# Masked attention and a top-1 expert layer on one core: the last heads by halves, the third half's rows through DRAM, a new written order

## The chip, the core and the metric

The kernel runs on one core of a Trainium2 chip. A core has a matrix engine (PE, TensorE, with its weight loader PEld), three others for vectors and scalars (DVE, VectorE; ACT, ScalarE; POOL, GpSimd) and a sync engine (SP) that only issues transfers. Each works through its own list of instructions in order, and semaphores make one wait for another. PE writes to PSUM, eight banks of 2 KB per partition; the rest works on SBUF. Transfers run on 16 DMA engines and are issued from the queues of SP, ACT and POOL. The metric is device time in microseconds.

## The reference

Attention on 2 batches of 8 heads, 768 positions of 64 numbers, where a query sees only the keys of its own bucket (six sign bits of a projection). Its output, 768 rows of 512 per batch, goes to a layer of 8 experts: each row to one expert, the argmax of a gate unless a local gate says to keep the expert of the row before.

```python
q_bits = (np.einsum('bhsd,dk->bhsk', q, proj) > 0)
mask = q_bucket[:, :, :, None] == k_bucket[:, :, None, :]
scores = np.where(mask, scale * np.matmul(q, k.transpose(0, 1, 3, 2)), -1e9)
attn = np.exp(scores - scores.max(-1, keepdims=True))
x = np.matmul(attn / (attn.sum(-1, keepdims=True) + 1e-9), v)    # then rows of 8*64
...
e = argmax(logits[b, s]) if s == 0 or local_gate[b, s] < 0.5 else prev_e
h = np.maximum(x[b, s] @ w1[e], 0.0)                             # 512 -> 1024
out[b, s] = p[e] * (h @ w2[e])                                   # 1024 -> 512
```

## The kernel before

**Attention.** Two heads make a pair; there are 8 pairs p (0 to 3 of batch 0, 4 to 7 of batch 1). The queries of a pair fall into two halves of 384, the keys into six tiles kt. For each pair `s1` makes scores for the row maxima (PE, then a reduction on DVE, L268), and `s2.p.kt.half` makes the scores again (PE, L259), with the exponential on ACT (L315). `pv.p.kt.half` multiplies with v (PE, L329), `flat` (L336) adds the term for queries without keys, and `padd` (L322, POOL or DVE) adds up the six exponentials of a half. `sa`/`sb` (L372, L381) turn these sums into denominators for both halves of a pair; in the last pair `sah`/`sbh` do it for one half, with 12 records of one column (L351). `ot`/`oth` copy pv's result to SBUF (ACT) and `ug` multiplies it with the identity and the gate's weights (PE, L414); DVE then normalises it into the row buffer xt and into gr, the gate's parts.

**Route.** The gate's sums (lg), seven small DVE operations (L488 to L495), a transpose `tk` (PE, L505), two scans over positions (DVE, L510 and L512: the expert that is kept, and the running count per expert), a transpose back `tb` (PE, L519) and some fifteen small operations give each row a slot. Rows are scattered by POOL to a DRAM buffer xs, 256 slots per expert (L551), 128 rows at a time. `step` advances this work, which is a generator.

**First expert.** Its 256 slots are not waited for in DRAM. For batch 0 they come from DRAM (`xa`, L639, then `rows`, PE, L708); rows of batch 1 are gathered by matmuls with a one-hot matrix: the third half (batch 1, first half) by `ohe`, `hle`, `ge`, the last half by `oh`, `gl` (L714, 24 matmuls of 256 columns each). `ready` splits the result into high and low parts x0H and x0L, as all products here are made of split operands. `hidden` is an expert's first layer (hps, L756), 24 matmuls for each of four tiles; the second layer is yps (L837).

**What sets the order.** Up to the first expert's input it is written out by hand: the string ORDER lists calls such as `pv.6.3.1`, and the table MOVED says which of two engines or queues a part takes (padd: 0 POOL, 1 DVE; hi: 0 ACT, 1 DVE, 2 POOL; lo: 0 DVE, 1 POOL; wl and split_l: 0 POOL, 1 DVE). From the second expert on a scheduler orders the instructions. For each expert it has eight weight tiles of 512 KB (`weights`, L791 the load, L793 the high part wh on ACT, L794 the low part wl on DVE), the rows (`xprep`: load xsl L800, eight transposes xps L804, xH on ACT L806, xL on DVE), and two scatters to out (L847). In expert 0 the call for expert 1's rows stands in the middle of the second layer, at t=1, i=2; its load is issued from POOL's queue, behind the small load PI.

Of the kernel before, what the change touches and what calls it, by code (L numbers as in the profile page):

```python
# [16 lines left out]
CAP = 256  # L17
# [44 lines left out]
padd.5.5.1 s2.6.3.0 s2.6.2.0 s2.6.4.1 s2.6.0.1 s2.6.2.1 wl.0 s2.6.1.1 padd.5.5.0 padd.6.2.0 s2.6.3.1 s1.7.4.1
padd.6.1.1 pv.6.0.0 pv.6.0.1 padd.6.3.0 pv.6.2.1 s1.7.5.1 s1.7.2.1 mf.6 s1.7.2.0 pv.6.1.1 pv.6.2.0 padd.6.4.0 pv.6.4.0
sa.5 ve.1 ma.7 mb.7 we.1 ug.4 sb.5 mc.7 padd.6.2.1 flat.6.0 flat.6.1 ug.5 mf.7 step.0 split_h.0 s2.7.2.0 s2.6.5.1
padd.6.3.1 we.2 ve.0 s2.7.0.0 s2.7.1.0 s2.6.5.0 padd.7.1.0 s2.7.3.0 padd.7.2.0 padd.6.4.1 padd.6.5.0 split_h.1
pv.6.4.1 pv.6.3.0 wh.2 padd.7.3.0 padd.6.5.1 pv.6.1.0 pv.6.5.0 we.4 pv.6.3.1 wh.1 pv.6.5.1 ot.6 s2.7.4.0 s2.7.2.1
padd.7.4.0 s2.7.1.1 s2.7.5.0 s2.7.0.1 sa.6 pv.7.0.0 flat.7.0 wl.2 step.0 split_l.0 we.5 split_l.1 padd.7.5.0 step.0
sb.6 wh.5 ug.6 xa.0 pv.7.2.0 pv.7.1.0 padd.7.1.1 padd.7.2.1 pv.7.4.0 pv.7.3.0 pv.7.5.0 sah.7.0 wl.1 oth.7.0 sbh.7.0
ugh.7.0 step.1 s2.7.3.1 s2.7.4.1 padd.7.3.1 padd.7.4.1 s2.7.5.1 xa.1 step.1 pv.7.0.1 flat.7.1 pv.7.2.1 padd.7.5.1
pv.7.4.1 pv.7.1.1 split_h.2 pv.7.3.1 step.1 pv.7.5.1 sah.7.1 wh.4 step.1 sbh.7.1 ohe oth.7.1 ugh.7.1 late step.2  # L70
rows.2 hle.0 split_h.3 split_l.2 rows.0 rows.1 hle.1 step.2 split_l.3 ge.0 rows.3 ge.1 ve.3 ge.2 step.2 oh step.2 wl.5
wl.4 ve.2 ge.3 gl.0 gl.1 ready.0 gl.2 gl.3 ready.1
"""

MOVED = {
    "bd": {(1, 0, 1): 1, (3, 0, 0): 1, (3, 0, 1): 1, (3, 1, 1): 1, (4, 0, 0): 1, (4, 1, 1): 1, (5, 0, 0): 1, (5, 0, 1): 1, (5, 1, 0): 1, (5, 1, 1): 1, (6, 0, 0): 1, (6, 0, 1): 1, (6, 1, 0): 1, (7, 1, 0): 1, (7, 1, 1): 1},
    "hi": {(3, 1): 1, (4, 1): 1, (5, 0): 1},
    "hle": {(1,): 1},
    "lo": {(0, 0): 1, (0, 1): 1, (1, 0): 1, (1, 1): 1, (2, 0): 1, (3, 1): 1, (4, 0): 1, (4, 1): 1, (5, 1): 1, (6, 0): 1, (7, 0): 1, (7, 1): 1},
    "lx": {(1, 1): 1, (2, 0): 1, (4, 0): 1, (5, 1): 1, (7, 0): 1},  # L80
    "padd": {(0, 1, 1): 1, (0, 4, 1): 1, (1, 3, 0): 1, (1, 5, 1): 1, (2, 2, 1): 1, (2, 4, 1): 1, (3, 1, 0): 1, (3, 4, 1): 1, (3, 5, 0): 1, (4, 1, 1): 1, (4, 4, 0): 1, (4, 5, 0): 1, (5, 1, 0): 1, (5, 5, 1): 1, (6, 5, 0): 1, (6, 5, 1): 1, (7, 1, 0): 1, (7, 1, 1): 1, (7, 2, 0): 1, (7, 2, 1): 1, (7, 3, 0): 1, (7, 3, 1): 1, (7, 4, 0): 1, (7, 4, 1): 1, (7, 5, 0): 1, (7, 5, 1): 1},
    "split_l": {(0,): 1, (1,): 1, (2,): 1, (3,): 1},
    "wl": {(0,): 1, (1,): 1, (2,): 1, (3,): 1, (4,): 1, (5,): 1},
}


LEFT = {0: (), 1: ()}
# [45 lines left out]
def tile_kernel(ctx, tc, qT, kT, v, proj, wg, w1, w2, cst, out):  # L133
    nc = tc.nc
    const = ctx.enter_context(tc.tile_pool(name="const", bufs=1))
    dram = ctx.enter_context(tc.tile_pool(name="dram", bufs=1, space=bass.MemoryType.DRAM))
    pvp = ctx.enter_context(tc.tile_pool(name="pvp", bufs=1, space=PSUM, reuse_waits="tile"))
    actx = ExitStack()
    ptp = actx.enter_context(tc.tile_pool(name="ptp", bufs=10))
    own = actx.enter_context(tc.tile_pool(name="own", bufs=1))  # L140
# [221 lines left out]
    def ot(p):  # L362
        for half in range(2):
            oth(p, half)
# [572 lines left out]
```

## Time and profile before

| | us |
|---|---|
| time, median of 3 runs (437.73 to 438.17) | 437.81 |
| the profiled execution | 437.44 |
| its span | 435.6 |
| PE busy | 420.4 (97%) |
| DVE busy | 286.2 (66%) |
| ACT busy | 207.1 (48%) |
| POOL busy | 175.6 (40%) |
| mean granted clock | 0.997 |

The span is the time from the first to the last instruction of the profile; the rest of the profiled execution's own time lies around it. Busy times are sums over the whole span and say little about one stage: attention takes the first 230 us, the route and the first expert's input the next 14, the experts the rest, one every 22.8 us at the end. Durations on PE overlap, since matmuls are pipelined; what one costs is the distance between starts.

### The profile page before, as it was taken

How to read it: one execution, taken by the hardware profiler on the slowest of the kernel's cores; microseconds unless marked ns; L12 is line 12 of the kernel's file. 1: busy time of each engine (PE TensorE's matmuls, PEld its weight loads, DVE VectorE, ACT ScalarE, POOL GpSimd, SP SyncE). 2: the span in 40 equal slices, each digit the busy share in tenths (PEclk: the TensorE clock that was granted, in tenths of full speed). 3: DMA queues.
4: the chain of work that ended last, by engine and by line, in shares of the span. 5: the costliest groups of instructions: out<-in, count | busy, mean ns of one | idle time of the engine just before them, and what ended most of it. 6: DMA issues, size and time to landing. Idle time of an engine off the chain costs nothing.

```text
span 435.6 us, 8104 instructions
## 1 busy us (share of the span) xinstructions
PE 420.4 (97%) x3206; PEld 328.6 (75%) x3206; DVE 286.2 (66%) x454; ACT 207.1 (48%) x288; POOL 175.6 (40%) x126
## 2 busy tenths in 40 slices
PE   7999999999999999999997998999999999999993
PEld 5665766747676675767656997989898989898992
DVE  3878858586665797779698865968574746464110
ACT  4444542715644364436532346756673746463110
POOL 4573886397579749792074212020000000000001
PEclk9999999999999999999999999999999999999998
DMA  8451224012122350203034179997777767740100
GB/s 267 117 169 31 89 78 129 19 42 87 45 80 66 110 175 5 63 2 110 2 147 169 55 244 367 362 325 256 251 260 242 227 216 239 241 154 2 38 2 32
DMA packets 42612, 60.08 MB, mean 138 GB/s; under 512 B 5431, under 2 KB 25129, under 8 KB 42572
## 3 DMA queue, kind: packets, MB, share of 16 engines
q1 hardware_dynamic: 38835, 50.14, 35.8%
q0 software_dynamic: 2432, 6.84, 4.2%
q10 hardware_dynamic: 1305, 2.57, 1.9%
q8 instruction: 26, 0.43, 0.4%
q14 instruction: 14, 0.11, 0.1%
HBM read 47.75 MB, written 11.56 MB: 136 GB/s over the span
## 4 chain that ended last, share of the span: by engine, by line
PE 49%; issue 40%; POOL 5%; DVE 1%; DMA 1%; ACT 1%; POOLq 0%; SPq 0%
PE s L259 25%; PE pv L329 15%; POOL out L847 4%; PE ug L414 3%; PE st L372 1%; PE hb L198 1%; POOL xs L551 1%; DMA xk<-kT 1%; PE pv L336 1%; PE st L381 1%; PE busy L605 1%; PE vt L584 0%; POOL xhl L646 0%; DMA PI<-xs 0%; PE st L351 0%
## 5 line engine op out<-in xcount | busy, mean ns | idle before, releaser
L268 DVE TENSOR_REDUCE mx<-s 128x2 f32<-128x768 f32 x96 | 88.8, 954 | 30.6 <-PE s L259 30.2
L794 DVE TENSOR_TENSOR wl<-st,wh 128x1024 fp32r<-128x1024 f32 x56 | 67.3, 1222 | 49.9 <-ACT wh L793 49.1
L315 ACT ACTIVATE pt<-s 128x768 f32<-128x768 f32 x96 | 71.6, 813 | 52.5 <-PE s L259 52.4
L322 POOL TENSOR_TENSOR sp<-sp,pt 128x768 f32<-128x768 f32 x44 | 82.1, 1877 | 26.9 <-DVE sp L322 20.2
L793 ACT ACTIVATE wh<-st 128x1024 fp32r<-128x1024 f32 x56 | 58.5, 1058 | 32.9 <-DMA st<-w 21.7
L259 PE MATMUL s<-hx 64*128 64x384 f32 x384 | 71.1, 365 | 0.5 <-DVE mx L268 0.3
L329 PE MATMUL pv<-pt,v 128*64 128x384 f32 x384 | 70.3, 496 | 0.0
L847 POOL DMA_INDIRECT out<-y,xsl x13 | 13.3, 1024 | 139.2 <-ACT y L840 139.2
L259 PE MATMUL s<-b,b 64*128 64x384 f32 x372 | 63.3, 334 | 0.6 <-ACT b L222 0.6
L259 PEld LDWEIGHTS s<-hx 64*128 64x128 f32 x384 | 36.4, 184 | 25.1 <-issue 8.7
L756 PE MATMUL hps<-xH,wh 128*128 128x256 f32 x224 | 53.8, 277 | 0.0
L756 PE MATMUL hps<-xH,wl 128*128 128x256 f32 x224 | 53.8, 277 | 0.0
L837 PE MATMUL yps<-wh,hH 128*128 128x512 f32 (+1 forms) x136 | 52.2, 384 | 0.0
L837 PE MATMUL yps<-wh,hL 128*128 128x512 f32 (+1 forms) x136 | 51.7, 380 | 0.0
L837 PE MATMUL yps<-wl,hH 128*128 128x512 f32 (+1 forms) x136 | 51.5, 379 | 0.0
L329 PEld LDWEIGHTS pv<-pt,v 128*64 128x64 f32 x384 | 24.2, 136 | 30.8 <-issue 29.9
L756 PEld LDWEIGHTS hps<-xH,wl 128*128 128x128 f32 x224 | 42.1, 188 | 0.3
L756 PEld LDWEIGHTS hps<-xH,wh 128*128 128x128 f32 x224 | 42.1, 188 | 0.3
L259 PEld LDWEIGHTS s<-b,b 64*128 64x128 f32 x372 | 35.5, 185 | 0.8 <-ACT b L222 0.8
L759 DVE SCALAR_TENSOR_TENSOR hL<-hps,hH 128x512 fp32r<-128x512 f32 x32 | 22.0, 687 | 19.3 <-ACT hH L758 19.3
L756 PE MATMUL hps<-xL,wh 128*128 128x256 f32 x224 | 34.6, 277 | 0.0
L259 PE MATMUL s<-hx,lx 64*128 64x384 f32 x192 | 32.7, 333 | 0.0
(204 smaller groups left out, 628.4 us busy)
## 6 DMA issues: line engine op xcount, KB each, us to landing
st<-w SPq DMA_DIRECT2D x56, 512.0 KB
xs<-z SPq DMA_DIRECT2D x8, 513.0 KB
st<-w SPq DMA_DIRECT2D x13, 256.0 KB
xsl<-xs SPq DMA_DIRECT2D x6, 514.0 KB
v<-v SPq DMA_DIRECT2D x12, 256.0 KB
xk<-kT SPq DMA_DIRECT2D x6, 384.0 KB
xq<-qT SPq DMA_DIRECT2D x5, 384.0 KB
xq<-qT ACTq DMA_DIRECT2D x3, 384.0 KB
```

The source lines that it names most:

```text
L259: nc.tensor.matmul(out=sc[:, h, 0:384], lhsT=w[r, cols[0]], rhs=x[r, cols[1]], tile_position=(64 * h, 0), start=first and n == 0, stop=las ...
L268: nc.vector.tensor_reduce(out=MX[p][:, kh, i // 3, :, i % 3], in_=sc[:, :, 0:384], axis=AX.X, op=ALU.max)
L315: nc.scalar.activation(out=pt.rearrange("p (a q) -> p a q", a=2), in_=sc[:, :, 0:384], func=ACTF.Exp, scale=0.125)
L322: eng.tensor_tensor(out=SP[p, h], in0=PT[p, 0, h] if kt == 1 else SP[p, h], in1=PT[p, kt, h], op=ALU.add)
L329: nc.tensor.matmul(out=PV[p][64 * h:64 * h + 64, half, 0:384], lhsT=V[b, kt][:, pp * 128 + 64 * h:pp * 128 + 64 * h + 64], rhs=PT[p, kt, h ...
L414: nc.tensor.matmul(out=t[:, half, j * 146:j * 146 + 146], lhsT=OT[p][:, q * 128:q * 128 + 128], rhs=iw[:, pp])
L756: nc.tensor.matmul(out=hps[:, k], lhsT=w, rhs=x, start=(k, n) in ends[0], stop=(k, n) in ends[1])
L759: LAST["DVE"] = nc.vector.scalar_tensor_tensor(out=hL, in0=hps, scalar=0.0, in1=hH.bitcast(F32), op0=ALU.max, op1=ALU.subtract).ins
L793: nc.scalar.activation(out=H, in_=st, func=ACTF.Copy)
L794: nc.vector.tensor_tensor(out=L, in0=st, in1=H.bitcast(F32), op=ALU.subtract)
L837: nc.tensor.matmul(out=yps[:, us], lhsT=h[:, k, ts], rhs=w[:, k, us], start=(n == 0), stop=(n == 23))
L847: i = nc.gpsimd.indirect_dma_start(out=dst, out_offset=bass.IndirectOffsetOnAxis(ap=idx, axis=0), in_=y[:, us], in_offset=None, bounds_che ...
```

## The change

- **pv.** The PSUM tile of a pair (two banks, one buffer) becomes one tile of one bank per half (two buffers).
- **Last pairs.** Pairs 6 and 7 go by halves: (6,0) and (7,0) first, then (6,1) and (7,1). Their sums are made by group, `sc` and `sd` for GROUPS, in place of sa.6, sb.6, sah, sbh. `pre` sums the gate's first six parts ahead.
- **Third half.** Its rows are scattered to DRAM early enough for `xa`; `ohe`, `hle`, `ge` (24 gathers) go. The matmuls of `rows` and `gl` share a helper `into`.
- **Route of the last half.** Scans in pieces of 256 and 128 columns (`sn`), back transposes and copies in two parts (`bk`, `cp`), the one-hot by parts (`oh.j`). The late normalisation moves from one DVE operation to six on ACT.
- **Expert 1's rows.** They are loaded by POOL's queue before PI (`rows1`), and `xprep` does them in two parts at t=1, i=3. Its PSUM tile has a pool of its own.
- **ORDER and MOVED** are new throughout. padd on DVE 26 → 37 of 80, hi on DVE 3 → 10, lo on POOL 12 → 16, wl on DVE 6 → 4.

Of ORDER one line is shown.

```diff
+GROUPS = (((6, 0), (7, 0)), ((6, 1),), ((7, 1),))
...
+pre.0 ugh.7.0 s2.6.5.1 s2.6.4.1 step.1 padd.6.4.1 pv.6.0.1 padd.6.5.1 pv.6.2.1 pv.7.0.1 step.1 split_l.0 s2.7.4.1
...
+    pvp = pctx.enter_context(tc.tile_pool(name="pvp", bufs=2, space=PSUM, reuse_waits="tile"))
...
-    def sah(p, half):
-        st = ps.tile([128, 2, 512], F32, tag="big", name="st")
-        ST[p, half] = st
-        terms = [SP[p, half]] + [PT[p, kt, half] for kt in LEFT[half]]
-        for h in range(2):
-            for j in range(3):
-                for n, x in enumerate(terms):
-                    nc.tensor.matmul(out=st[:, 0, 3 * h + j:3 * h + j + 1], lhsT=x[:, h * 384 + 128 * j:h * 384 + 128 * j + 128],
-                                     rhs=ones[:, 0:1], start=(n == 0), stop=(n == len(terms) - 1))
-
-    def sbh(p, half):
-        d = ST[p, half][:, 1, 0:6].rearrange("p (h j) -> p h j", h=2)
-        nc.vector.scalar_tensor_tensor(out=d, in0=DN[p][:, half], scalar=1e-9,
-                                       in1=ST[p, half][:, 0, 0:6].rearrange("p (h j) -> p h j", h=2), op0=ALU.add, op1=ALU.add)
-        if p not in DR:
-            DR[p] = smp.tile([128, 2, 2, 3], F32, tag="r", name="r")
-        nc.vector.reciprocal(out=DR[p][:, half], in_=d)
-
-    def ot(p):
-        for half in range(2):
-            oth(p, half)
+        nc.scalar.activation(out=OT[p][:, half * 384:half * 384 + 384], in_=PV[p, half][:, 0:384], func=ACTF.Copy)
+
+    def sc(g):
+        ST["g", g] = st = ps.tile([128, 2, 512], F32, tag="big", name="st")
+        n = 0
+        for p, half in GROUPS[g]:
+            for h in range(2):
+                nc.tensor.matmul(out=st[n:n + 32, 0, 0:384], lhsT=ones, rhs=SP[p, half][:, h * 384:h * 384 + 384], tile_position=(0, n))
+                n += 32
+        ss = smp.tile([128, 384], F32, tag="ss", name="ss", bufs=1)
+        nc.scalar.activation(out=ss[0:n], in_=st[0:n, 0, 0:384], func=ACTF.Copy)
+        NF["g", g] = ss
+
+    def sd(g):
+        st, ss, m = ST["g", g], NF["g", g], len(GROUPS[g])
+        n = 64 * m
+        for j in range(3):
+            nc.tensor.transpose(st[:, 1, j * n:j * n + n], ss[0:n, j * 128:j * 128 + 128], idf[0:n, 0:n])
+        d = st[:, 1, 384:384 + 6 * m].rearrange("p (a h j) -> p a h j", a=m, h=2)
+        r = smp.tile([128, 2, 2, 3], F32, tag="r", name="r")
+        for a, (p, half) in enumerate(GROUPS[g]):
+            nc.vector.scalar_tensor_tensor(
+                out=d[:, a], in0=DN[p][:, half], scalar=1e-9,
+                in1=st[:, 1, 0:3 * n].rearrange("p (j a h r) -> p a h j r", j=3, a=m, h=2)[:, a, :, :, 0],
+                op0=ALU.add, op1=ALU.add)
+            DR[p, half] = r[:, a]
+        nc.vector.reciprocal(out=r[:, 0:m].rearrange("p a h j -> p (a h j)"), in_=d.rearrange("p a h j -> p (a h j)"))
...
+        def scan(i, a, c1, c2):
+            h = halves[i]
+            o, p = slice(384 * h + c1, 384 * h + c2), 384 * h + c1 - 1
+            if a == 0:
+                V_.tensor_tensor_scan(out=E[:, o], data0=KS[i][:, c1:c2], data1=cs[0:8, 3:4].to_broadcast([8, c2 - c1]),
+                                      initial=E[:, p:p + 1] if h or c1 else 0.0, op0=ALU.subtract, op1=ALU.is_lt)
+            else:
+                V_.tensor_tensor_scan(out=C[:, o], data0=E[:, o], data1=E[:, o], op0=ALU.add, op1=ALU.max,
+                                      initial=C[:, p:p + 1] if h or c1 else CU[0] if b else cs[0:8, 152:153])
+
+        def back(q1, q2):
+            for a, src in enumerate((E, C)):
+                for q in range(q1, q2):
+                    o = 384 * halves[0] + 128 * q
+                    nc.tensor.transpose(tb[:, a, q * 8:q * 8 + 8], src[:, o:o + 128], idf[0:8, 0:8])
+
+        def copy(q1, q2):
+            V_.tensor_copy(out=EC[b][:, :, q0 + q1:q0 + q2], in_=tb[:, :, q1 * 8:q2 * 8].rearrange("p a (q e) -> p a q e", e=8))
...
-    def ohe():
-        OHE.append(onehot("sp", 0))
...
-    def hle(i):
-        c = slice(256 * i, 256 * i + 256)
-        hl = [ptp.tile([128, 3, 256], F32R, tag="pt", name="xhl") for _ in range(2)]
-        HLE.append(hl)
-        nc.scalar.activation(out=hl[0], in_=XT[1][:, 0:3, c], func=ACTF.Copy)
-        (nc.vector, nc.gpsimd)[moved("hle", i)].tensor_tensor(
-            out=hl[1], in0=XT[1][:, 0:3, c], in1=hl[0].bitcast(F32), op=ALU.subtract)
...
+    def into(c, cols, **kw):
+        i = c // 2
+        if not xt0:
+            for k in range(2):
+                xt0[k], XN[k] = pvp.tile([128, 512], F32, tag="pv", name="xt0").rearrange("p (c n) -> p c n", c=2), 0
+        nc.tensor.matmul(out=xt0[i][:, c % 2, cols], start=XN[i] == 0, stop=XN[i] == 15, **kw)
+        XN[i] += 1
...
+    def gl(c, j):
+        for k in range(2):
+            into(c, slice(0, 256), lhsT=XHL[k][:, j, 128 * c:128 * c + 128], rhs=OH[0][:, j])
...
+    def late():
+        t, r = LATE.pop()
         for j in range(3):
-            for k in range(2):
-                nc.tensor.matmul(out=xt0[c // 2][:, c % 2], lhsT=hl(k, j), rhs=oh[:, j], start=False,
-                                 stop=(last and c % 2 == 1 and j == 2 and k == 1))
-
-    def ge(c):
-        gather(OHE[0], c, lambda k, j: HLE[c // 2][k][:, j, 128 * (c % 2):128 * (c % 2) + 128])
-
-    def gl(c):
-        gather(OH[0], c, lambda k, j: XHL[k][:, j, 128 * c:128 * c + 128], True)
-
-    def oh():
-        OH.append(onehot("oh", 3))
-
-    def late():
-        LATE.pop()()
+            for h in range(2):
+                nc.scalar.activation(out=XT[1][:, 3 + j, 384 + 64 * h:448 + 64 * h], in_=t[:, 1, 146 * j + 64 * h:146 * j + 64 * h + 64],
+                                     func=ACTF.Copy, scale=r[:, h, j:j + 1])
...
+        rows1 = xload(mp, xs[CAP:2 * CAP], nc.gpsimd)
+        nc.gpsimd.dma_start(out=PI, in_=xs[0:CAP, 512:514].rearrange("(t p) c -> p t c", p=128))
...
-    def xprep(slots, queue=nc.sync, after=None):
-        xsl = mp.tile([128, 2, 514], F32, tag="xsl", name="xsl")
-        with tc.issue_after(after) if after else nullcontext():
-            queue.dma_start(out=xsl, in_=slots.rearrange("(t p) c -> p t c", p=128))
-        xps = pvp.tile([128, 4, 256], F32, tag="pv", name="xps")
-        for c in range(4):
-            for t in range(2):
-                nc.tensor.transpose(xps[:, c, 128 * t:128 * t + 128], xsl[:, t, 128 * c:128 * c + 128], idf)
+    def xprep(xsl, parts=1):
+        xps = px.tile([128, 4, 256], F32, tag="xps", name="xps")
         xH, xL = (wide(mp, [128, 4, 256], n, XOFF, 64) for n in ("xH", "xL"))
-        LAST["x"] = (nc.scalar.activation(out=xH, in_=xps, func=ACTF.Copy).ins,
-                     nc.vector.tensor_tensor(out=xL, in0=xps, in1=xH.bitcast(F32), op=ALU.subtract).ins)
-        return xsl[:, :, 512:514], xH, xL
+        LAST["x"] = []
+        for part in range(parts):
+            cs_ = slice(4 // parts * part, 4 // parts * (part + 1))
+            for c in range(4)[cs_]:
+                for t in range(2):
+                    nc.tensor.transpose(xps[:, c, 128 * t:128 * t + 128], xsl[:, t, 128 * c:128 * c + 128], idf)
+            LAST["x"] += (nc.scalar.activation(out=xH[:, cs_], in_=xps[:, cs_], func=ACTF.Copy).ins,
+                          nc.vector.tensor_tensor(out=xL[:, cs_], in0=xps[:, cs_], in1=xH[:, cs_].bitcast(F32), op=ALU.subtract).ins)
+            yield xsl[:, :, 512:514], xH, xL
...
-                if after and (t, i) == (1, 2):
-                    nxt = mid()
                 for k in range(2):
+                    if after and (t, i) == (1, 3):
+                        nxt = next(prep)
```

In the places that follow, rows of the order are of one engine. First PE around the end of attention, before: st is a sum, ug the projection, xt the first expert's rows being put together, tk and tb the route's transposes.

```order
L351 MATMUL st<-ones,sp 128x1 x6
L414 MATMUL ug<-iw,ot 128x146 x3
L708 MATMUL xt_3001<-cs,xa 128x128 x2
L708 MATMUL xt_3010<-cs,xa 128x128 x4
L505 MATMUL tk<-cs,gr_115 8x128 x3
L714 MATMUL xt_3010<-oh,xhl 128x256 x6
L708 MATMUL xt_3001<-cs,xa 128x128 x2
L714 MATMUL xt_3010<-oh,xhl 128x256 x6
L714 MATMUL xt_3001<-oh,xhl 128x256 x6
L519 MATMUL tb<-cs,rE 128x8 x3
L519 MATMUL tb<-cs,rC 128x8 x3
L714 MATMUL xt_3001<-oh,xhl 128x256 x6
```

And now, from sd.1 on:

```order
L360 MATMUL st<-cs,ss 128x64 x3
L350 MATMUL st<-sp,ones 32x384 x2
L419 MATMUL ug<-iw,ot 128x146 x3
L360 MATMUL st<-cs,ss 128x64 x3
L419 MATMUL ug<-iw,ot 128x146 x3
L517 MATMUL tk<-cs,gr_115 8x128 x3
L722 MATMUL xt_3009<-cs,xa 128x128 x2
L534 MATMUL tb<-cs,rE 128x8 x2
L534 MATMUL tb<-cs,rC 128x8 x2
L722 MATMUL xt_3009<-cs,xa 128x128 x2
L534 MATMUL tb<-cs,rE 128x8
L534 MATMUL tb<-cs,rC 128x8
L722 MATMUL xt_3010<-cs,xa 128x128 x4
```

The gathers of the third half (xhl) are gone, and with them the one-column sum; two half projections and three small sums stand ahead of tk. The matmuls on xa now stand behind tk and ahead of tb.

Second, ACT at expert 1, before. wh are weight tiles of expert 1 in the order of their loads by number (3404, 3410, 3416, 3422 of w1, 3544, 3550 of w2), xH its rows, y the output of expert 0.

```order
L793 ACTIVATE wh_3410<-st_3408 128x1024
L840 ACTIVATE y_3337<-yps_3312,PI_112 128x512
L806 ACTIVATE xH_3366<-xps_3357 128x1024
L793 ACTIVATE wh_3416<-st_3414 128x1024
L793 ACTIVATE wh_3544<-st_3542 128x1024
L840 ACTIVATE y_3382<-yps_3342,PI_112 128x512
L793 ACTIVATE wh_3422<-st_3420 128x1024
L793 ACTIVATE wh_3550<-st_3548 128x1024
L758 ACTIVATE hH_3451<-hps_3426 128x512
```

And now (3396, 3402, 3408, 3414 of w1; 3536, 3542, 3548, 3554 of w2):

```order
L826 ACTIVATE wh_3402<-st_3400 128x1024
L880 ACTIVATE y_3329<-yps_3304,PI_112 128x512
L826 ACTIVATE wh_3536<-st_3534 128x1024
L839 ACTIVATE xH_3354<-xps_3353 128x512
L826 ACTIVATE wh_3542<-st_3540 128x1024
L880 ACTIVATE y_3374<-yps_3334,PI_112 128x512
L826 ACTIVATE wh_3548<-st_3546 128x1024
L839 ACTIVATE xH_3354<-xps_3353 128x512
L826 ACTIVATE wh_3408<-st_3406 128x1024
L826 ACTIVATE wh_3554<-st_3552 128x1024
L826 ACTIVATE wh_3414<-st_3412 128x1024
L789 ACTIVATE hH_3443<-hps_3418 128x512
```

xH comes in two halves. The first tile of w2 has moved ahead of the first half, and the second and third ahead of the second half; the third and fourth tile of w1 come later. DVE's order of wl and xL is the same.

Third, PE at the same place now (before, the eight transposes stood in the middle of the second layer, 12 yps ahead of the first hps):

```order
L877 MATMUL yps<-wh,hL 128x512
L787 MATMUL hps<-xH,wh 128x256
L787 MATMUL hps<-xH,wl 128x256
L787 MATMUL hps<-xH,wh 128x256
L787 MATMUL hps<-xH,wl 128x256
L787 MATMUL hps<-xH,wh 128x256
L787 MATMUL hps<-xH,wl 128x256
L787 MATMUL hps<-xH,wh 128x256
L787 MATMUL hps<-xH,wl 128x256
L838 MATMUL xps<-cs,xsl 128x128 x4
L787 MATMUL hps<-xH,wh 128x256
L787 MATMUL hps<-xH,wl 128x256
```

Eight matmuls use the first half of xH, then four transposes make the second half, and all that follows waits for it.

## Rows read from the trace of the kernel before

**Rows 1.** Windows (start:end, PE, PEld, DVE, ACT, POOL busy, clock, DMA share, GB/s)

```profile
220.00:230.00 10.00, 9.80 (x74) 5.96 (x73) 9.10 (x22) 4.05 (x7) 5.96 (x5) 1.00 0.36 134
...
260.00:270.00 10.00, 8.75 (x48) 7.20 (x47) 4.83 (x5) 5.09 (x6) 1.31 (x1) 1.00 1.03 354
```

**Rows 2.** Timeline of PE near 100 us (start, duration, line, shapes, count, [idle before])

```profile
100.45 0.44 PE L259 MATMUL s<-hx 64*128 64x384 f32 x2
100.73 0.34 PE L259 MATMUL s<-b,b 64*128 64x384 f32 x2
```

**Rows 3.** Timeline of PE, sums, pv runs and projection

```profile
211.41 0.85 PE L372 MATMUL st<-sp,ones 128*32 128x384 f32 x8
212.20 0.87 PE L329 MATMUL pv<-pt,v 128*64 128x384 f32 x4
...
214.59 1.66 PE L414 MATMUL ug<-iw,ot 128*128 128x146 f32 x12
216.17 3.45 PE L329 MATMUL pv<-pt,v 128*64 128x384 f32 x20
219.55 1.50 PE L351 MATMUL st<-ones,sp 128*128 128x1 f32 x12
220.91 0.99 PE L414 MATMUL ug<-iw,ot 128*128 128x146 f32 x6
```

**Rows 4.** Timeline of PE, last pv to first expert

```profile
229.41 0.87 PE L329 MATMUL pv<-pt,v 128*64 128x384 f32 x4
230.21 1.50 PE L351 MATMUL st<-ones,sp 128*128 128x1 f32 x12
...
232.67 1.71 PE L708 MATMUL xt<-cs,xa 128*128 128x128 f32 x12
235.81 0.49 PE L505 MATMUL tk<-cs,gr 128*8 128x128 f32 x3 [1.43 <-DVE gr L495]
...
239.98 0.35 PE L519 MATMUL tb<-cs,rE 8*128 8x8 f32 x3
...
241.35 0.38 PE L714 MATMUL xt<-oh,xh 128*128 128x256 f32 x1
...
244.32 0.86 PE L756 MATMUL hps<-x0H,b 128*128 128x256 f32 x6
```

**Rows 5.** Timeline of DVE, the two scans of the last half

```profile
236.91 1.00 DVE L510 TENSOR_TENSOR_SCAN rE<-tk,rE,cs 8x384 f32<-8x384 f32 x1
237.95 2.01 DVE L512 TENSOR_TENSOR_SCAN rC<-rE,rC 8x384 f32<-8x384 f32 x1
```

**Rows 6.** Timeline of SP, loads of the scattered rows

```profile
229.57 0.81 SPq L639 DMA_DIRECT2D xa<-xs  x2
```

**Rows 7.** DMA issues from 233 to 240 us (queue, count, us to landing)

```profile
xs<-xt,rsi POOLq DMA_INDIRECT x3, 3.4
```

**Rows 8.** DMA issues from 253 to 272 us

```profile
xsl<-xs POOLq DMA_DIRECT2D x1, 514.0 KB, 8.7
```

**Rows 9.** Timeline of PE, second layer of expert 0, then expert 1

```profile
255.39 0.39 PE L837 MATMUL yps<-wh,hH 128*128 128x512 f32 x1
...
265.05 1.09 PE L804 MATMUL xps<-cs,xsl 128*128 128x128 f32 x8 [1.25 <-DMA xsl<-xs]
...
268.77 0.28 PE L756 MATMUL hps<-xH,wh 128*128 128x256 f32 x1
```

**Rows 10.** Timeline of ACT in the same stretch

```profile
264.16 1.06 ACT L793 ACTIVATE wh<-st 128x1024 fp32r<-128x1024 f32 x1 [4.50 <-DMA st<-w]
...
266.18 1.02 ACT L806 ACTIVATE xH<-xps 128x1024 fp32r<-128x1024 f32 x1 [0.39 <-PE xps L804]
...
268.51 1.06 ACT L793 ACTIVATE wh<-st 128x1024 fp32r<-128x1024 f32 x1 [0.36 <-DMA st<-w]
```

**Rows 11.** Line 322, padd, on both engines (count: ns min/median/max)

```profile
L322 POOL TENSOR_TENSOR sp<-sp,pt x44: 1802/1834/2507, 25.6 to 197.5; 128x768 f32<-128x768 f32 x44
L322 DVE TENSOR_TENSOR sp<-sp,pt x20: 921/953/2220, 54.2 to 228.2; 128x768 f32<-128x768 f32 x20
```

More of the change, by code (lines that the diff above doesn't have):

```diff
@@ L65 @@
[L65 to L69, printed above, removed]
@@ L335, in flat @@
         b, pp = divmod(p, 4)
-        nc.tensor.matmul(out=PV[p][:, half, 0:384], lhsT=VS[b][:, pp * 128:pp * 128 + 128],
+        nc.tensor.matmul(out=PV[p, half][:, 0:384], lhsT=VS[b][:, pp * 128:pp * 128 + 128],
                          rhs=Fl[:, half * 384:half * 384 + 384], start=False, stop=False)
@@ L427, in norm @@
                 nc.vector.tensor_tensor(
-                    out=GR[b][:, half * 3:half * 3 + 3, :, 2 * pp:2 * pp + 2].rearrange("p j e h -> p j h e"),
+                    out=(sums(half)[:, :, :, 1:3] if b and last else
+                         GR[b][:, half * 3:half * 3 + 3, :, 2 * pp:2 * pp + 2]).rearrange("p j e h -> p j h e"),
                     in0=src[:, :, 128:146].rearrange("p j (h e) -> p j h e", h=2),
@@ L512, in route @@
-            V_.tensor_tensor_scan(out=C[:, o], data0=E[:, o], data1=E[:, o], op0=ALU.add, op1=ALU.max,
-                                  initial=C[:, 383:384] if h else CU[0] if b else cs[0:8, 152:153])
-        yield
-        for i, h in enumerate(halves):
-            for a, src in enumerate((E, C)):
-                for j in range(3):
-                    q = 3 * i + j
-                    nc.tensor.transpose(tb[:, a, q * 8:q * 8 + 8], src[:, 384 * h + 128 * j:384 * h + 128 * j + 128], idf[0:8, 0:8])
@@ new lines, in back @@
+        def back(q1, q2):
[5 more added lines that the diff above has]
+            V_.tensor_copy(out=EC[b][:, :, q0 + q1:q0 + q2], in_=tb[:, :, q1 * 8:q2 * 8].rearrange("p a (q e) -> p a q e", e=8))
+        KS = [tk[0:8, i, 0:384] for i in range(len(halves))]
+        if halves == (1,):
+            PIECES.extend((scan, back, copy))
+            yield
+        else:
+            for i in range(len(halves)):
+                K = smp.tile([8, 384], F32, tag="rK", name="rK")
+                nc.scalar.activation(out=K, in_=KS[i], func=ACTF.Copy)
+                KS[i] = K
+                for a in range(2):
+                    scan(i, a, 0, 384)
+            yield
+            back(0, n)
+            if not b:
+                yield
+            copy(0, n)
+            if b:
+                yield
@@ L601, in busy @@
         if not IDLE:
-            IDLE.append(pvp.tile([128, 2, 512], F32, tag="pv", name="busy"))
+            IDLE.extend(pvp.tile([128, 512], F32, tag="pv", name="busy") for _ in range(2))
         for _ in range(n):
             for i in range(2):
-                nc.tensor.matmul(out=IDLE[0][:, i, 0:384], lhsT=Fl[64 * i:64 * i + 64, 0:128],
+                nc.tensor.matmul(out=IDLE[i][:, 0:384], lhsT=Fl[64 * i:64 * i + 64, 0:128],
                                  rhs=Fl[64 * i:64 * i + 64, 0:384], tile_position=(64 * i, 0))
```

216 lines of the change are left out of this document (111 added, 105 removed).

## The prediction

> **What bounds the kernel now.** I read the windows first, then PE's timeline, then the timelines of the engines that PE waits for. PE fills nearly all of every window from 20 to 230 us; the one in [rows 1] has 9.80 of 10 us, with DVE at 9.10 beside it, and a granted clock of 1.00. So up to the last pv of attention the time is PE's own work, and DVE is close to being a second bound. I call T the end of the last pv, 230.2 [rows 4]. From T to the first matmul of the first expert, at 244.32, there is a chain: sums, projection, the route on DVE, tk (PE), two scans (DVE), tb, the one-hot, 24 gathers, hps. It takes 14.1 us, in which PE waits little only because other gathers fill it. The first layer of the first expert ends at S, 255.39 [rows 9]. Behind it PE waits 1.25 us for the second expert's rows, and then runs to the end without waits worth naming. So the end moves by what three places give or take: T, the way from T to hps, and the way from S into expert 1. Each us there is a us at the end.
>
> **Attention, up to T.** Removed before T: sa.6 (0.85), the one-column sum sah.7.0 (1.36 from start to next start), and half of ug.6, which now falls behind T (1.66 less 0.99, 0.67) [rows 3]; sb.6 goes and sd.0 of the same kind comes. Added: sc.0, eight records as sa had (0.85), and sc.1, half of that (0.42). 2.88 less 1.27 is 1.6 us. The new order also joins pv into 40 runs where there were 45. A run of 4 records takes 0.87 and one of 20 takes 3.45 [rows 3], 0.645 per four and 0.22 beside; the first score behind a run has 0.10 more than the next [rows 2], part of it within the 0.22. I take 0.2 per run, 1.0 us, between 0.5 and 1.6.
>
> What could give it back is DVE. In all, 11 more of the additions (padd) stand on DVE, seven of the hi copies, while reductions stay; less for the gathers' one-hot. Worked out with 0.953 us an addition [rows 11], DVE's work to T grows by some 10 us in 228, and POOL's shrinks by more. Over the last 40 us I walked the new order by hand: behind the last s1, PE has 41.7 us of its own up to T. DVE's last addition for the group of halves (7,0) ends 0.75 us before PE asks for it, the route's tk is ready 1.1 us before, the third half's scans 0.9 us before. All hold, but with the fast price of an addition; the mean, 1.14, would eat each of these. I count 0.5 us of new waits, bounds 0 and 2. T moves by -1.6 - 1.0 + 0.5 = -2.1, to 228.1.
>
> [...]
>
> **From T to hps.** Before: T to tk 5.6, tk to hps 8.5 [rows 4]. What leaves the first stretch is one one-column sum (1.5), the one-hot of the third half and the late normalisation from DVE; what comes is a second pair's projection and normalisation, and two wl subtractions of an addition's shape, 0.95 each [rows 11]. I make it 5.8, bounds 5.0 and 7.0. In the second, POOL's split of the third half is gone, and the second scan with it falls from 2.01 to 1.00 [rows 5]; scanning in pieces of 256 and 128 columns moves the same columns, with a copy and a tb between. The 24 gathers at the end stay (241.35 to 244.32, 2.97), and the one-hot ahead of them too. 8.5 less 1.0, less 0.5 to 0.8 of a subtraction that stood ahead of the scans: 6.8, bounds 6.0 and 7.8. Together 12.6 against 14.1, -1.5.
>
> The third half's way through DRAM is hidden, by my walk: its gate column is ready at T-3.1, three scatters leave by T-0.4, they took 3.4 before [rows 7], and xa, issued at 229.57 before and used at 232.67 without a wait [rows 4, 6], takes at most 2.7 more. That is T+5.7 to T+6.7; the matmuls on xa stand ahead of tb, which could start at T+7.7. So hps starts at 228.1 + 12.6 = 240.7, 3.6 earlier.
>
> **From S into expert 1.** The rows of expert 1 are now loaded behind the last scatter, ahead of PI, before S rather than 0.9 after it; they took 8.7 us [rows 8]. They will be there when PE asks, and 1.25 us go. But ACT's order changes. Before, xH followed two weight tiles and y. Now the fifth tile (the first of w2) comes ahead of the first half of xH, and the sixth, y and the seventh ahead of the second half. PE's own work from S to hps is 13.38 - 1.25 = 12.1 [rows 9]; with the eight matmuls on the first half, at 0.12 each (the 24 gathers of that width), it reaches the second half's at S+13.1. The second tile landed at S+8.8, the fifth at S+13.1, when ACT had waited 0.36 for it [rows 10]. The DMA engines moved 354 GB/s there [rows 1], and the rows' 514 KB stood among them, 1.5 us at that pace; with these out of the way I take the fifth 1.5 us earlier, S+11.6 (bounds 10 and 13.1). Then ACT: 1.06, half an xH 0.55, 1.06, y 0.65, the seventh tile 1.06 (landed by S+14.6 if tiles follow each other by 1.5), half an xH 0.55: S+16.6. PE waits 3.5 where it waited 1.25: +2.3, bounds +0.6 and +4.0.
>
> [...]
>
> Later experts differ in the order of prefetches only, at places where PE never waited; 0.
>
> **Sum.** -2.1 - 1.5 + 2.3 = -1.3. The profiled execution took 437.44 (span 435.6 and 1.84 around it), the median is 437.81; I put the same difference on it: 436.5.
>
> **Rivals.**
> *The weights come early.* If hidden(0)'s loads end sooner and the fifth tile lands at S+10, ACT's chain ends at S+15.0 and the wait is 1.9, +0.65 for the place. With no new waits in attention either: -2.6 - 1.5 + 0.65 = -3.4, 434.4. For it: DMA stands nearly idle in the 2 us ahead of S. Against: the tiles of expert 1 are asked for at S as before.
> *DVE becomes the bound of attention.* Place: the four halves at the end, where DVE had 0.9 us to spare in 10 [rows 1] and takes on five more additions. Price: at the mean price instead of the median, 17 additions make 3.2 us, of which the margins of 0.75 to 1.1 hide one; other stages with as little room add as much again, 4 us of waits in place of 0.5. Then 437.8 + 2.2 = 440.0. It is slower than before from 2.6 us of waits. For it: the long additions of [rows 11]. Against: POOL is nearly empty of additions in those stages.
> *The third half's rows are late.* If the scatters take 5 us and xa 3, or the gate column is 1.5 us late, the rows block tb, and each us beyond T+7.7 shifts hps by one. With 1.5 us: 438.0, no change. For it: scatter, wait, load follow each other with nothing between; against: the margin of 1 to 2 us.
>
> **How the numbers follow.** Forecast 0.45, its own range 435.0 to 438.0; early weights 0.2; DVE the bound 0.2; rows late 0.15. A difference under 0.2%, 0.88 us, can't be told from none. Of the forecast two thirds lie below 436.9; with early weights and a little of the third rival that makes faster 0.54. Slower takes most of the DVE case and a little of the others, 0.19; 0.27 stays for the same. The range reaches from beyond the early weights to near the DVE case: 433.4 to 439.6.
>
> **What would show it.** In the changed profile: T near 228.1 with no PE wait over 0.5 behind DVE or ACT before it; tk at T+5.8 and hps at T+12.6; xa's matmuls without an idle time named DMA; the first transpose of expert 1 without a wait, and then PE idle for 2 to 5 us ahead of hps, released by ACT's second xH. If that last wait is under 1 us, the time is near 434 and my order of landings is wrong; if T comes later than 230, the DVE case is true.

## The result, and the profile after

| | before | after |
|---|---|---|
| median of 4 runs, us | 437.82 (437.73 to 438.17) | 443.83 (442.11 to 446.76) |
| profiled execution, us | 437.44 | 442.11 |
| its span, us | 435.6 | 440.2 |
| mean granted clock of the profile | 0.997 | 0.984 |

The ratio is 1.0136, interval 1.0087 to 1.0186: slower by 6.0 us, where 436.5 was forecast and the range ended at 439.6. The profiled execution is the fastest of the four. Its span is 4.6 longer, and divides so (S is the first yps of expert 0, 258.39 after):

| | before | forecast | after |
|---|---|---|---|
| T, end of the last pv | 230.2 | 228.1 | 232.2 |
| T to hps of expert 0 | 14.1 | 12.6 | 15.25 |
| hps to S | 11.07 | as before | 10.95 |
| S to the end of the span | 180.2 | 182.5 | 181.8 |

Windows of after (start:end, PE, PEld, DVE, ACT, POOL busy, granted clock, DMA share, GB/s) in attention and where [rows 1] stood:

```profile
140.00:150.00 10.00, 7.54 (x54) 3.93 (x54) 4.01 (x5) 3.45 (x5) 4.72 (x4) 0.83 0.00 1
220.00:230.00 10.00, 10.00 (x77) 5.80 (x75) 8.60 (x22) 4.94 (x8) 5.57 (x4) 1.00 0.49 157
260.00:270.00 10.00, 10.00 (x46) 7.90 (x44) 3.73 (x11) 3.88 (x5) 1.33 (x1) 1.00 1.05 354
```

And in stretches of 2 us, where the clock is below 1.00:

```profile
146.00:148.00 2.00, 2.00 (x16) 0.65 (x16) 0.96 (x1) 0.26 (x1) 0.00 (x0) 0.52 0.01 4
148.00:150.00 2.00, 2.00 (x11) 0.40 (x6) 1.13 (x2) 0.63 (x1) 0.00 (x0) 0.62 0.00 0
...
238.00:240.00 2.00, 1.20 (x4) 0.87 (x4) 1.85 (x3) 0.66 (x2) 0.00 (x0) 0.56 1.05 334
240.00:242.00 2.00, 2.00 (x10) 1.56 (x9) 1.13 (x3) 0.00 (x0) 0.00 (x0) 0.50 0.61 234
242.00:244.00 2.00, 2.00 (x11) 1.95 (x10) 1.48 (x8) 0.00 (x0) 0.00 (x0) 0.50 0.00 0
244.00:246.00 2.00, 2.00 (x14) 2.00 (x14) 1.79 (x11) 0.22 (x1) 0.00 (x0) 0.73 0.00 0
```

Of before, the first window:

```profile
140.00:150.00 10.00, 10.00 (x78) 6.81 (x79) 7.81 (x18) 4.20 (x6) 7.36 (x7) 1.00 0.19 66
```

Two things are new: PE idles for 2.46 us in the middle of attention, where its longest wait in before was 0.57 (from 20 to 230 us), and the granted clock falls twice to about 0.50.

**The gap at 143 us.** PE's timeline (start, duration, what, [idle before and what ended it]):

```profile
145.61 0.44 PE L260 MATMUL s<-hx 64*128 64x384 f32 x2 [2.46 <-ACT pt L316]
```

ACT's, whose exponential it waits for:

```profile
144.75 1.51 ACT L316 ACTIVATE pt<-s 128x768 f32<-128x768 f32 x2 [2.62 <-POOL sp L323]
```

And POOL's, whose addition the exponential waits for:

```profile
134.78 5.92 POOL L611 TENSOR_TENSOR va<-va,v 128x512 f32<-128x512 f32 x4
...
141.12 1.84 POOL L323 TENSOR_TENSOR sp<-pt 128x768 f32<-128x768 f32 x1
142.91 1.81 POOL L323 TENSOR_TENSOR sp<-sp,pt 128x768 f32<-128x768 f32 x1
```

Read upwards: scores wait for PSUM, which an exponential on ACT reads and has to empty; it waits for a buffer; the buffer is freed by an addition on POOL (padd.4.3.0, at 142.91), which stands behind all of vsum.1 (four of its five additions are the first row, and a memset follows) and another padd. Behind the gap come 4 us at 0.52 and 0.62: 2 × 0.48 + 2 × 0.38 = 1.7 us lost to the clock, by estimate. 2.46 and 1.7 make up the 4.1 by which T is later than forecast.

**The tail.** PE, for [rows 4]:

```profile
232.19 0.40 PE L360 MATMUL st<-cs,ss 64*128 64x64 f32 x3
...
237.57 0.49 PE L517 MATMUL tk<-cs,gr 128*8 128x128 f32 x3 [2.00 <-DVE gr L508]
238.85 1.57 PE L722 MATMUL xt<-cs,xa 128*128 128x128 f32 x4 [0.80 <-DMA xa<-xs]
240.36 0.38 PE L534 MATMUL tb<-cs,rE 8*128 8x8 f32 x2
...
244.07 0.56 PE L722 MATMUL xt<-oh,xh 128*128 128x256 f32 x1
244.43 0.41 PE L722 MATMUL xt<-oh,xl 128*128 128x256 f32 x1
...
245.20 0.28 PE L722 MATMUL xt<-oh,xl 128*128 128x256 f32 x1
...
247.44 1.59 PE L787 MATMUL hps<-x0H,b 128*128 128x256 f32 x12
```

tk comes at T+5.4 (forecast 5.8). From tk to hps it is 9.9, not 6.8: much of it runs at about half clock (0.50 from 240 to 244), where a gather matmul takes 0.41 against 0.28 from 245 on.

**Expert 1.** PE, for [rows 9]:

```profile
258.39 0.39 PE L877 MATMUL yps<-wh,hH 128*128 128x512 f32 x1
...
268.00 0.60 PE L838 MATMUL xps<-cs,xsl 128*128 128x128 f32 x4
...
270.42 0.39 PE L787 MATMUL hps<-xH,wh 128*128 128x256 f32 x1 [0.42 <-ACT xH L839]
...
271.80 0.66 PE L838 MATMUL xps<-cs,xsl 128*128 128x128 f32 x4 [0.19 <-DVE xL L840]
273.38 0.39 PE L787 MATMUL hps<-xH,wh 128*128 128x256 f32 x1 [0.92 <-ACT xH L839]
...
307.19 1.06 PE L838 MATMUL xps<-cs,xsl 128*128 128x128 f32 x8 [0.72 <-DMA xsl<-xs]
```

ACT, for [rows 10]; the first row is the fifth tile:

```profile
268.82 1.06 ACT L826 ACTIVATE wh<-st 128x1024 fp32r<-128x1024 f32 x1 [2.64 <-DMA st<-w]
269.79 0.58 ACT L839 ACTIVATE xH<-xps 128x512 fp32r<-128x512 f32 x1
...
272.73 0.59 ACT L839 ACTIVATE xH<-xps 128x512 fp32r<-128x512 f32 x1
```

The rows are there without a wait, and both halves of xH then come late, as forecast; a wait of 0.72 for expert 3's rows, which the prediction had not foreseen, stands behind (expert 2's rows are transposed at 283.49 without a wait).

### The profile page after: what moved, and what is told of

It reads as the page before. It is cut to its first block, busy times and chain, and to the rows that moved or that the text cites. A ratio compares the mean times of both kernels' runs of the same rounds, so it can differ in the third digit from the quotient of the medians.

```text
span 440.2 us, 8053 instructions
## 1 busy us (share of the span) xinstructions
PE 421.0 (96%) x3172; PEld 326.9 (74%) x3172; DVE 289.9 (66%) x463; ACT 204.6 (46%) x288; POOL 168.9 (38%) x121
## 3 DMA queue, kind: packets, MB, share of 16 engines
q10 hardware_dynamic: 1005, 2.01, 1.4%
## 5 line engine op out<-in xcount | busy, mean ns | idle before, releaser
L316 ACT ACTIVATE pt<-s 128x768 f32<-128x768 f32 x96 | 72.7, 815 | 46.9 <-PE s L260 39.7
L323 POOL TENSOR_TENSOR sp<-sp,pt 128x768 f32<-128x768 f32 x32 | 60.0, 1887 | 34.1 <-DVE sp L323 29.8
L330 PE MATMUL pv<-pt,v 128*64 128x384 f32 x384 | 68.8, 494 | 0.0
L323 DVE TENSOR_TENSOR sp<-sp,pt 128x768 f32<-128x768 f32 x32 | 33.0, 1041 | 0.5 <-ACT pt L316 0.2
```

The lines of the kernel that those rows point to most:

```text
L316: nc.scalar.activation(out=pt.rearrange("p (a q) -> p a q", a=2), in_=sc[:, :, 0:384], func=ACTF.Exp, scale=0.125)
L323: eng.tensor_tensor(out=SP[p, h], in0=PT[p, 0, h] if kt == 1 else SP[p, h], in1=PT[p, kt, h], op=ALU.add)
L330: nc.tensor.matmul(out=PV[p, half][64 * h:64 * h + 64, 0:384], lhsT=V[b, kt][:, pp * 128 + 64 * h:pp * 128 + 64 * h + 64], rhs=PT[p, kt, h ...
```

## The experiments

Theory one: the place of padd.4.3.0 behind vsum.1, with the slow clock behind its gap, costs 4 us. Theory two: in the tail the removed gathers had kept PE at work, and without them the clock falls. The rival to both is that the new handling of expert 1's rows (later place, two parts) does the harm. The three do not exclude one another. Ratios are to the kernel before, on the same chip, with 95% intervals; medians carry range and number of runs.

**The addition ahead of vsum.1.**

```diff
-... s1.5.2.1 vsum.1 hp.7 ... bd.7.1.1 padd.4.3.0 s1.6.4.0 ...
+... s1.5.2.1 padd.4.3.0 vsum.1 hp.7 ... bd.7.1.1 s1.6.4.0 ...
```

> The changed kernel with one addition on POOL (pair 4, key tile 3, first half) ahead of the six operations that add up v of batch 1, not behind them. Theory: the exponential at 144.75 had waited for this addition's buffer, PE for the exponential (2.46 us), and the granted clock fell to 0.52 behind that wait. So the wait goes, the clock stays at 1.00 from 140 to 160 us, and the last pv ends 4.1 us earlier, at 228.1: 438.0 us against 442.1 for the changed kernel's profiled run. Rival 1, the fall of the clock has nothing to do with the wait: 2.5 us, 439.6. Rival 2, POOL's order is not the cause: 442 or more, with the wait still there.

Measured: 439.48 (437.39 to 441.55, 9), ratio 1.0049 [1.0029, 1.0069]; 4.35 less than after. Its window there:

```profile
140.00:150.00 10.00, 10.00 (x84) 6.22 (x81) 6.96 (x16) 4.49 (x7) 4.91 (x5) 1.00 0.01 2
```

The gap is gone, the clock stays at 1.00 there, and T is 228.1. The first theory holds; the kernel is still not faster than before.

**Unused matmuls in the tail.** Five ahead of tk and three behind it, of the width of 384 columns, into the unused second bank of tk's tile; alone, and with the addition moved.

```diff
+    def keep(t, n):
+        for _ in range(n):
+            nc.tensor.matmul(out=t[:, 1, 0:384], lhsT=VS[1][:, 0:128], rhs=Fl[:, 0:384])
...
+        keep(tk, 5 if last else 0)      # ahead of the transposes tk; 3 more behind them
```

> The changed kernel with eight more matmuls of 384 columns whose result is not used, five ahead of the last half's transpose tk and three behind it, where PE idled 2.0 and 0.9 us. Theory: the clock of 0.50 from 238.3 to 245 comes from this idling and costs the tail 3 us. So the clock stays at 1.00 from 235 to 250, the first expert starts 12.3 us after the last pv and not 15.25, and the time is 439.1 though PE has 2.6 us more to do. Rival: the tail waits for the rows through DRAM and for DVE, the slow matmuls are hidden; the first expert starts 14.5 to 15.3 us after the last pv, time 441.4 to 442.5.

> Both edits together. Theory: both gains add, clock 1.00 throughout up to 420 us, last pv at 228.1, first expert at 240.4, time 435.1, faster than before by 0.6%. Rival (clock a side matter in both places): 439 or more, no faster than before.

Measured: alone 442.62 (439.07 to 442.8, 5), ratio 1.011 [1.0083, 1.0137], which can't be told from after; with the addition moved 437.04 (435.63 to 439.55, 10), ratio 0.9989 [0.9966, 1.0011]. Alone, they miss the 439.1 of their theory. The second differs from the addition alone, its interval lies below, by some 2.4 us; 435.1 was expected. The five fill 1 of the 2 us (tk still waits 1.05), and the clock still reached 0.50 in both profiles. Where the 2.4 us come from, the profiles do not show: T to hps is 14.5 here and 14.1 in the profile of the addition alone, which is the fastest of its nine executions.

The profile with the matmuls alone also splits the 4.1 of the first theory: there the gap at 143 us stood, but the clock did not fall behind it, and T was 230.3, 2.2 later than with the addition moved.

**The kernel before without its gathers.** The 24 gathers of the third half go from the written order, so the first expert's input lacks the rows of that half; nothing else changes.

```diff
-... split_l.3 ge.0 rows.3 ge.1 ve.3 ge.2 step.2 oh ... ve.2 ge.3 gl.0 ...
+... split_l.3 rows.3 ve.3 step.2 oh ... ve.2 gl.0 ...
```

> The kernel before without the 24 matmuls that gather the third half's rows for the first expert (those rows are left out of the first expert's input, nothing else changes; the operations that prepare them stay). Theory: these matmuls hid nothing but they kept PE at work between tk and tb; without them PE idles some 3.5 us, the clock falls to 0.50 for 5 us or more, the first expert starts at 246 to 247 instead of 244.3 and the time is 439 to 440, slower with less work. Rival: the clock does not fall, the first expert starts at 244.0 to 244.4, time 437.2 to 437.5.

Measured: 439.04 (438.56 to 440.83, 10), ratio 1.0037 [1.0012, 1.0061]: less work, and slower. Its PE timeline, where the gathers stood:

```profile
238.88 0.35 PE L519 MATMUL tb<-cs,rE 8*128 8x8 f32 x3 [1.15 <-DVE rE L510]
240.91 0.48 PE L519 MATMUL tb<-cs,rC 8*128 8x8 f32 x3 [1.68 <-DVE rC L512]
```

And its windows:

```profile
234.00:236.00 2.00, 2.00 (x11) 2.00 (x11) 1.93 (x10) 0.43 (x1) 1.17 (x2) 0.50 0.35 132
...
242.00:244.00 2.00, 1.77 (x8) 1.77 (x9) 1.83 (x11) 0.00 (x1) 0.00 (x0) 0.50 0.00 0
244.00:246.00 2.00, 2.00 (x11) 2.00 (x11) 1.68 (x6) 0.82 (x2) 0.00 (x0) 0.50 0.00 0
```

PE idles by pieces there, and the clock behind is 0.50. The fall at 234 stands ahead of the gathers' place, though, and is not shown to come from their absence. The mean clock over the ten runs is 0.985, against 0.995 for before on that chip. So theory two is supported in so far as the gathers' absence goes with a lower clock and a longer time; by what way is not shown.

**More unused matmuls**, ten and five, with the addition moved; and as a control seven in the kernel before, ahead of its last tk.

> As the kernel with both edits, with ten unused matmuls ahead of tk instead of five and five behind it instead of three: the five had filled only 1.0 us of the 2.1 that PE idled there, and the clock still fell, to 0.50 at 237 us for 3.5 us. Theory: with PE at work up to tk the clock stays at 1.00 from 225 to 250 us in the profile, the first expert starts 12.5 us after the last pv instead of 14.4, mean clock over the runs 0.996 to 0.997 (0.9945 with five), time 435.0 to 436.0. Rival: it is the small matmuls of tb and of the rows that bring the clock down, not the idling; then it falls again behind 236 us and the time stays at 437.

> Control: the kernel before with seven such unused matmuls ahead of its last tk, where PE idles 1.4 us. Theory: its clock does not fall there (mean 0.995 over 24 runs, most of the lost part at the end of the span), so nothing is won: 437.5 to 438.2, ratio within 0.2% of 1. Rival: unused matmuls help any version by about as much as they helped the changed one (1.7 us and more): 436 or less.

Measured: 437.82 (436.17 to 440.55, 10), ratio 1.0005 [0.998, 1.0029], no better than with five and three (435 to 436 was expected); the control 437.53 (436.43 to 441.15, 10), ratio 1.0004 [0.9979, 1.0029], no gain. In the profile with ten and five, the slowest of its ten executions, the clock is 1.00 from 220 to 260, and hps comes at 241.07:

```profile
227.79 0.40 PE L360 MATMUL st<-cs,ss 64*128 64x64 f32 x3
...
233.09 0.49 PE L523 MATMUL tk<-cs,gr 128*8 128x128 f32 x3 [0.16 <-DVE gr L512]
233.33 1.12 PE L484 MATMUL tk<-Fl,VS 128*128 128x384 f32 x5
...
241.07 1.10 PE L794 MATMUL hps<-x0H,b 128*128 128x256 f32 x8
...
264.79 0.39 PE L794 MATMUL hps<-xH,wh 128*128 128x256 f32 x1 [1.16 <-ACT xH L846]
...
269.56 0.39 PE L794 MATMUL hps<-xH,wh 128*128 128x256 f32 x1 [2.73 <-ACT xH L846]
```

DVE's first scan in the same profile:

```profile
234.49 0.74 DVE L531 TENSOR_TENSOR_SCAN rE<-tk,rE,cs 8x256 f32<-8x256 f32 x1 [1.46 <-PE tk L484]
```

T to hps is 13.3, and 0.9 of it the experiment's own: the scan starts 1.40 behind tk, since it waits for the five matmuls into tk's tile, where it was 0.53 in after. Without them it would be 12.4, an estimate from these rows. But the gain is lost behind S: 3.9 us of waits for xH, and behind the longer of them the clock fell a third time, which after's profile does not have:

```profile
270.00:272.00 2.00, 2.00 (x14) 2.00 (x13) 2.00 (x4) 2.00 (x3) 0.00 (x0) 0.66 0.86 284
272.00:274.00 2.00, 2.00 (x12) 2.00 (x11) 2.00 (x3) 0.34 (x1) 0.00 (x0) 0.50 0.85 269
```

That is 1.7 us more by estimate, and expert 3's rows cost another 1.36. From S to the span's end it is 186.6 us, against 181.8 in after. That brought up the rival.

**Expert 1's rows in one part**, at the place that they had before (t=1, i=2), still loaded early: with the addition moved and the ten and five matmuls; with the addition alone; and with nothing else. The edit undoes place and halving together, and no run tells them apart.

```diff
-        prep = xprep(xnext(mid), 1 if not after else 2) if mid else None
+        prep = xprep(xnext(mid), 1) if mid else None
...
-                    if after and (t, i) == (1, 3):
+                    if after and (t, i, k) == (1, 2, 0):
```

> The same, and the second expert's rows are transposed and split in one part at t=1, i=2 again, so that ACT and DVE have the order of the kernel before there (rows, then the third tile of w1). Theory of the forecast: the order costs 0.7 us net (second half of xH behind w2's second and third tile); with the old order the first matmul of expert 1 comes 13.2 us after the first expert's first layer, limited by the rows' landing at 9.5, where with two parts all but eight matmuls came at 15.0: 0.8 us faster than the run beside it. Rival: the rows, not ACT's order, are what PE waits for; no difference or slower.

> The changed kernel with the addition moved ahead (as in the run with that edit alone, 439.48) and with expert 1's rows done in one part at t=1, i=2 as before; no unused matmuls. If the new place of expert 1's rows costs 3.6 us whenever T to hps ends, this takes 435.9. The rival: in a slow tail the second layer's weights have more time, so that the waits for xH are small (0.9 and 1.3 us in the changed kernel's profile, against 2.7 and 1.2 with the unused matmuls), and then it takes 438.5 to 439. In either case hps of expert 0 comes at T+14, with a granted clock of about .50 behind tk.

> The changed kernel with that last edit alone: the wait at 143 us and the slow tail are both there. By the first theory 443.8 - 3.6 = 440.2; by the rival 442.9 to 443.3. Either way it stays above the kernel before's 437.5, since the wait of 2.5 us and what follows it are not touched.

| this edit with | median (range, runs) | ratio to before |
|---|---|---|
| the addition and ten and five matmuls | 434.21 (433.81 to 435.72, 5) | 0.9918 [0.9864, 0.9972] |
| the addition | 434.73 (434.65 to 436.12, 5) | 0.9929 [0.9903, 0.9956] |
| nothing else | 439.95 (438.55 to 440.71, 10) | 1.0044 [1.0022, 1.0066] |

The edit is worth 3.6, 4.8 and 3.9 us beside the medians of the same kernels without it (of the last two on other chips); the rival, that a slow tail would hide its price, fails. (That rival was argued from waits of 0.9 and 1.3 us; the rows of after have 0.42 and 0.92.) Windows of the kernel with the addition (its S is 254.18), where expert 1 is prepared and behind:

```profile
255.00:285.00 30.00, 30.00 (x189) 26.77 (x188) 23.27 (x31) 21.27 (x25) 2.99 (x2) 1.00 1.02 348
285.00:310.00 25.00, 25.00 (x163) 22.62 (x162) 14.91 (x15) 12.62 (x16) 3.02 (x3) 1.00 0.88 297
```

PE fills both, and from S to the span's end it is 178.6 us, 3.2 less than after and 1.6 less than before. The first two rows beat both kernels; between them the unused matmuls can't be told from nothing. The addition and the rows together take 9.1 us off after, 443.83 to 434.73, where alone they take 4.35 and 3.9: more than the 6.0 by which after is slower than before.

The tail is not mended by any of this. T to hps is 15.35 in the profile with the addition, and 14.8 in the one with ten and five matmuls besides, where before had 14.1. In the latter PE has no wait over 0.18 from 227 to 242 us, and its clock falls all the same:

```profile
238.00:240.00 2.00, 2.00 (x11) 2.00 (x11) 1.86 (x11) 0.22 (x1) 0.00 (x0) 0.50 0.00 0
```

So filling the waits did not secure the clock there, and what brings it down in the tail stays open.

## Why the prediction was wrong

**T, at 228.1: failed, by the term "0.5 us of new waits, bounds 0 and 2".** I walked the last 40 us of attention and let the rest stand on sums of work per engine. The wait came at 143 us, from POOL's order and not from DVE's load: 2.46. The other terms came out right as a sum: with that one addition moved T is 228.1, and 227.6 to 227.9 in four more profiles that have the edit. None of them was measured by itself, and before's own T was 231.1 in two more profiles with its attention, so an agreement within 0.1 is in part luck.

**The clock was no term of the sum.** A granted clock of 1.00 in [rows 1] was read as a given, and its fall was put at nothing without a reason. It fell behind the gap (1.7 us) and behind tk. It was 0.52 and 0.56 behind these two waits, of 2.46 and 2.00 us, but it also fell where no long wait is listed, as the last section shows. What makes it fall, no run shows.

**T to hps, 12.6: the steps right, at full clock.** tk at T+5.4 for 5.8. tk to hps took 9.9 at half clock, 8.75 with the addition moved, and in the profile at full clock 8.0 less 0.9: 7.1 for 6.8. In every other profile of the changed kernel T to hps took 14.1 to 15.4, no less than before, so the forecast gain of 1.5 was not had. "PE waits little only because other gathers fill it" stood in the prediction's first part; that they must then be replaced by something was not followed up.

**The third half's rows: partly the rival.** xa made PE wait 0.80, at T+5.9 to T+6.7, the late end of the forecast. tb, which needed the first two scans (done at T+7.4), began at T+8.2 behind matmuls on xa at a granted clock of 0.56 (238 to 240); of the 0.8 between these two, no run tells the share of the rows from that of the clock. The scans on DVE:

```profile
238.10 0.74 DVE L524 TENSOR_TENSOR_SCAN rE<-tk,rE,cs 8x256 f32<-8x256 f32 x1 [0.67 <-PE tk L517]
238.87 0.74 DVE L527 TENSOR_TENSOR_SCAN rC<-rE,rC 8x256 f32<-8x256 f32 x1
239.53 0.45 DVE L524 TENSOR_TENSOR_SCAN rE<-tk,rE,cs 8x128 f32<-8x128 f32 x1
240.01 0.47 DVE L527 TENSOR_TENSOR_SCAN rC<-rE,rC 8x128 f32<-8x128 f32 x1
```

Beside [rows 5], the second scan indeed lost its 2.01: four pieces take 2.4 in all. That POOL's split had made it 2.01, as the sum took it, no run shows by itself: in before the split ran beside it (L646, 237.39 to 239.14), where the same scan took 1.01 with no POOL operation beside it (at 200.21 and 202.16), and in after no POOL operation ran beside the four pieces.

**S into expert 1, +2.3: the mechanism right, +0.8 at its place.** 1.25 went; 1.53 of waits came at expert 1. The next expert's transposes, behind expert 1's first layer, show what the place gave, S+24.3 before and S+25.1 after:

```profile
279.69 1.03 PE L804 MATMUL xps<-cs,xsl 128*128 128x128 f32 x8
283.49 1.04 PE L838 MATMUL xps<-cs,xsl 128*128 128x128 f32 x8
```

The other half of the +1.6 from S to the end came by expert 3's rows, where the sum had 0; that 1.6 lies near 2.3 is in part luck. S to the end is 3.2 longer than with the rows in one part, 2.3 of it at expert 1 (S+25.1 against S+22.8); the 0.9 that the listed waits don't cover was not traced. The fifth tile came at S+10.4 (forecast 11.6, bounds 10 and 13.1), 2.7 earlier than before where the sum took 1.5 for the rows' own bytes, a share that no run shows by itself; the second half of xH was ready at S+14.9 (16.6). In the profile where hps came early the waits were 3.9, against 3.5 forecast. That experts behind it would lose nothing was wrong by the 0.72: the load of expert 3's rows stands in SP's queue behind weight tiles, and was issued at S+44.4, against S+40.5 with the rows in one part.

**DVE as the bound of attention: not seen.** The additions on DVE, now 32 of this form, are as fast as in [rows 11]:

```profile
L323 DVE TENSOR_TENSOR sp<-sp,pt x32: 922/950/2120, 36.9 to 230.6; 128x768 f32<-128x768 f32 x32
```

Their mean is 1041 ns, where it was 1143 before. Counting those of form sp<-pt, three of 37 took over 0.96 us (1.78 to 2.12), where it was four of 26 in before (1.49 to 2.22). Beside each of the seven a TENSOR_TENSOR on POOL was running that had started 0.26 to 1.16 us earlier; of the others, at 0.92 to 0.96 us, five had one beside them, each started later than the addition. The 11 more additions thus brought no more long ones; what makes one long, no run shows.

The forecast 436.5 is 7.3 below the median: in the profile T (4.1) and the tail (2.65) are over, hps to S (0.1) and expert 1 (0.7) under, 5.9 in all; the other 1.4 are the executions behind the fastest, whose mean clocks are 0.977 to 0.983 against 0.984.

## What to carry to other kernels

When a written order changes throughout, walk every stretch for what stands ahead of each instruction that frees a buffer, not only the stretch that was rebuilt: one addition queued behind others, on an engine with time to spare, cost 4.35 us here. Before work is taken out of a wait, ask what PE does there instead, and price the rest of the chain at the clock of 0.50 that the tail showed here, as a rival. And where a copy moves behind weight tiles that come from DRAM, ask when the tiles land: here ACT waited 2.64 us for the tile ahead of the first half of xH; that part of the change, place and halving together, cost 3.6 to 4.8 us, and without it and the misplaced addition the kernel is 0.7% faster than before.

## What the runs showed of the hardware

- A gap was not always followed by a fall of the clock. With the unused matmuls alone the same gap of 2.5 us at 143 us stood in the profile, and the clock stayed at 1.00 from 140 to 150; in after it fell to 0.52. Before waited 1.43 ahead of tk [rows 4] without a fall; 2.00 at that place was followed by one in all four profiles that had it.
- It fell without a long wait too: in before without its gathers it was 0.50 from 234 to 236, behind the 12 sums of one column and six of the projection; no wait of PE is listed from 228 to 236. Nor is one over 0.18 ahead of the 0.50 in the profile with ten and five unused matmuls and the rows in one part.
- The early load of expert 1's rows landed in half the time of [rows 8]:

```profile
xsl<-xs POOLq DMA_DIRECT2D x1, 514.0 KB, 4.3
```
